# An FNet and MLP-mixer kernel: even-odd split of the feature transform, token-weight copies moved behind the fold of batch 1, fourth operand sum ahead of the third

## Chip, cores and metric

The kernel runs on one core of one Trainium2 chip. Times are device microseconds (us) of one execution. One run of the kernel before took 877 us at a clock of 0.66; it is left out.

## The reference

```python
# x (8, 3008, 256); w_tok1 (3008, 256); w_tok2 (256, 3008); w_ch1 (256, 1536); w_ch2 (1536, 256)
X = np.fft.fft(np.fft.fft(x, axis=1), axis=2).real        # token and feature transform
h = np.maximum(X.transpose(0, 2, 1) @ w_tok1, 0.0) @ w_tok2
u = X + h.transpose(0, 2, 1)
out = u + np.maximum(u @ w_ch1, 0.0) @ w_ch2
```

## The kernel before

TensorE does both transforms and all products in fp16. The work of a batch on the way to its output:

- **fold**: symmetric sums and differences of x, which halve the feature transform. VectorE does it for batches 0 and 1, GpSimd for the others, in steps placed between other work.
- **pz, z**: stage of the token transform. **pw, w**: the feature transform, 12 pairs of matmuls a batch. **py, pt, pu**: the rest of the token transform and the token MLP, up to `ut`.
- **mm1** (`pc`, ReLU into `c1`) and **mm2**, the channel MLP. A batch has six chunks of 512 tokens; a chunk has 12 "slots" (one per block of 128 hidden channels), here called slot 0 to 71 of a batch. mm2 uses seven block products instead of eight for most chunks; for that VectorE makes four operand sums `s` of 1536 fp16 elements a row per chunk.

The parts that the change and the argument touch (cuts marked):

```python
def fold(b, eng):                                   # 17 steps
    ...
    for t0, t1 in ((13, 17), (9, 13), (5, 9), (1, 5)):
        ...
        tt(fa[:], xp[:, t, 1:129], rv[:, :, 255:127:-1], AT.add, eng)
        yield
        tt(fb[:], rv[:, :, 1:129], xp[:, t, 255:127:-1], AT.add, eng)
        tt(eo[:, t, 0:1], xp[:, t, 0:1], rv[:, :, 0:1], AT.add, eng)
        yield
        tt(eo[:, t, 1:129], fa[:], fb[:], AT.add, eng)
        yield
        tt(eo[:, t, 129:256], fa[:, :, 0:127], fb[:, :, 0:127], AT.subtract, eng)
        yield
    ...
# feature transform, in front(b)
for g in range(NG):                                 # 12
    pw = ps_f("pw")
    nc.tensor.matmul(pw[:, 0:257], lhsT=zg[:, 1, g], rhs=td1[:], start=True, stop=False)
    nc.tensor.matmul(pw[:, 0:129], lhsT=zg[:, 0, g], rhs=td0[:], start=False, stop=True)
    copy(g % 2 == 0 and b == 0, w[:, g, :], pw[:, 0:257])
    yield
...
sum_at = {0: 1, 1: 2, 4: 3, 5: 4}                   # place in the chunk: which operand sum
places = {0: 0, 1: -1, 2: 1, 4: 2, 6: 3, 7: 4, 9: 5, 11: 6}   # which product
...
        if b == 0:
            if 12 <= slot < 24:
                take(fold1, 1 + slot % 2)           # fold of batch 1, on VectorE
            if slot == 21 and BB > 2:
                load_x(2)
            if slot in (22, 24, 26, 28):            # token weights into their later place, on GpSimd
                ...
                G.tensor_copy(out=w2r[:, th, 32 * hb:32 * hb + 32, 0:NQ], in_=...)
        ...
        if slot in fold_at:                         # fold of batch b + 2, on GpSimd
            ...
            G.tensor_copy(out=hold[:], in_=pbox[4][:, 0, 0, 0:1])   # waits for the fourth sum
            take(fold2, fold_at[slot])
```

`hold` is a copy of one column. Its only use is that GpSimd waits there until VectorE has the last sum of the chunk, so that the two don't meet.

## Time and profile before

| | before |
|---|---|
| median of the 3 runs | 604.52 us (603.12 to 604.69) |
| span of the profiled run | 601.9 us |
| first steady mm1 matmul, last matmul (starts) | 33.89 us, 597.80 us |
| TensorE from the one to the other | 563.91 us |

The last row is the one to think with: ahead of it lies a start-up that fills TensorE only in part, and behind it 4.1 us of last eviction (the copy of a result out of PSUM) and store. First, busy time by stretch (columns: window, its length, then busy us of PE, PEld, DVE, ACT, POOL, each with its instructions; granted clock, DMA share, GB/s):

```profile
64.00:110.00 46.00, 46.00 (x483) 32.66 (x482) 36.11 (x69) 28.11 (x56) 19.13 (x24) 1.00 0.32 73
...
180.00:250.00 70.00, 70.00 (x789) 50.88 (x787) 53.09 (x99) 47.00 (x93) 23.43 (x32) 1.00 0.56 91
```

TensorE has no idle time in either. Next, the timeline of GpSimd's token-weight copies and of the first operand sums that VectorE makes (start, us, engine, line, operation):

```profile
57.90 5.59 POOL L817 COPY w2r<-w2n 128x1504 f16<-128x1504 f16 x4
...
68.35 0.95 DVE L90 TENSOR_TENSOR s<-c 128x1536 f16<-128x1536 f16 x1
```

The copies end at 63.49 us, 4.9 us before the kernel's first sum. A sum takes 0.95 us. Last, the timeline around the third sum (`s<-c`) and the product that reads it (`pa<-t3w,s`), late in batch 0:

```profile
100.64 0.95 DVE L90 TENSOR_TENSOR s<-c 128x1536 f16<-128x1536 f16 x1
...
102.11 0.95 DVE L90 TENSOR_TENSOR s<-c,s 128x1536 f16<-128x1536 f16 x1
...
103.20 0.83 PE L650 MATMUL pa<-t3w,s 128*128 128x128 f16 x12
```

The third sum is there 1.6 us before its product.

### The profile page before, as it was taken

The numbers are of one execution on the slowest core, as the hardware profiler recorded it, in microseconds if no ns is written. First come the engines' busy times: TensorE is split into PE (matmuls) and PEld (weight loads), VectorE is DVE, ScalarE is ACT, GpSimd is POOL, SyncE is SP. The second block draws the span as 40 slices with busy tenths as digits, with TensorE's granted clock in tenths as the row PEclk, the third lists the DMA queues.
The fourth block names the chain that finished last, engine by engine and source line by source line (L and its number), as shares of the span: only waits on it lengthen the run. The fifth ranks groups of instructions, "written<-read, shape, count | busy, mean of one in ns | idle before, by whom it ended". The sixth has DMA issues, their size and how long they took to land.

```text
span 601.9 us, 15073 instructions
## 1 busy us (share of the span) xinstructions
PE 586.4 (97%) x6229; PEld 420.1 (70%) x6229; DVE 438.1 (73%) x884; ACT 387.2 (64%) x751; POOL 184.6 (31%) x260
## 2 busy tenths in 40 slices
PE   3999999999999999999999999999999999999997
PEld 2656676677667776667767777667766777666775
DVE  8778669566887578765888658856688757866663
ACT  8765665586657865577656866468665876546662
POOL 8443245603552143503336033450454000000000
PEclk9899999999999999999999999999999999999999
DMA  8994713671239812592336942376124533233433
GB/s 156 210 180 81 169 37 67 131 120 45 54 71 149 119 45 59 103 157 54 83 70 98 138 78 54 67 157 102 36 54 81 93 56 56 50 88 74 94 71 90
DMA packets 83381, 55.66 MB, mean 92 GB/s; under 512 B 53747, under 2 KB 80051, under 8 KB 82547
## 3 DMA queue, kind: packets, MB, share of 16 engines
q1 hardware_dynamic: 76816, 36.82, 32.6%
q0 software_dynamic: 6176, 17.63, 16.5%
q8 instruction: 48, 0.79, 0.5%
q10 hardware_dynamic: 320, 0.26, 0.2%
q14 instruction: 21, 0.16, 0.1%
HBM read 35.26 MB, written 24.64 MB: 100 GB/s over the span
## 4 chain that ended last, share of the span: by engine, by line
PE 95%; ACT 2%; DVE 2%; DMA 1%; issue 0%; DVEq 0%
PE pc L600 40%; PE pa L650 18%; PE pb L650 14%; PE pu L504 7%; PE po L705 5%; PE pt L533 3%; PE py L476 2%; PE pw L450 2%; PE pz L424 2%; DMA xm<-in_x_dram,ix 1%; PE pw L452 1%; ACT z L97 1%; ACT tts L97 0%; DVE yt L90 0%; DVE eo L90 0%; ACT w L97 0%
## 5 line engine op out<-in xcount | busy, mean ns | idle before, releaser
L97 ACT ACTIVATE c<-pc 128x512 f16<-128x512 f32 (+1 forms) x553 | 311.6, 590 | 154.7 <-PE pc L600 130.3
L600 PE MATMUL pc<-ut,wc 128*128 128x512 f16 (+1 forms) x1152 | 312.7, 374 | 0.3 <-DVE ut L90 0.3
L650 PEld LDWEIGHTS <-s 128*128 128x128 f16 x1968 | 123.4, 98 | 37.8 <-DVE s L90 1.5
L600 PEld LDWEIGHTS <-wc 128*128 128x128 f16 x1152 | 98.0, 98 | 57.0 <-issue 2.2
L650 PEld LDWEIGHTS <-c 128*128 128x128 f16 x1476 | 93.1, 97 | 27.8
L90 DVE TENSOR_TENSOR q<-pa,uT 128x256 f32<-128x256 f32 x123 | 53.1, 432 | 45.3 <-PE pa L650 44.5
L90 DVE TENSOR_TENSOR s<-c 128x1536 f16<-128x1536 f16 x82 | 78.8, 961 | 5.5 <-ACT c L97 5.5
L826 POOL COPY hold<-s 128x1 f16<-128x1 f16 x23 | 4.3, 188 | 251.3 <-DVE s L90 251.3
L90 DVE TENSOR_TENSOR osb<-pb,q 128x256 f32<-128x256 f32 x123 | 52.1, 424 | 33.4 <-PE pb L650 29.7
L90 DVE TENSOR_TENSOR ut<-pu,yt 128x512 f16<-128x512 f32 (+1 forms) x96 | 64.2, 674 | 2.3 <-PE pu L504 2.1
L90 POOL TENSOR_TENSOR eo<-fa,fb 96x512 f16<-96x512 f16 (+1 forms) x48 | 54.2, 1151 | 0.0
L504 PE MATMUL pu<-w2r,uu 128*128 128x512 f16 (+1 forms) x168 | 50.0, 379 | 0.0
L97 ACT ACTIVATE w<-pw 128x257 f16<-128x257 f32 x90 | 34.6, 385 | 10.6 <-PE pw L452 9.3
L90 DVE TENSOR_TENSOR s<-c,s 128x1536 f16<-128x1536 f16 x41 | 38.9, 949 | 0.0
L90 DVE TENSOR_TENSOR s<-s,c 128x1536 f16<-128x1536 f16 x41 | 38.8, 947 | 0.0
L705 PE MATMUL po<-wc,c 128*128 128x256 f16 x288 | 35.4, 273 | 0.0
L90 DVE TENSOR_TENSOR osb<-pa,uT 128x256 f32<-128x256 f32 x41 | 17.4, 425 | 23.7 <-PE pa L650 23.7
L650 PE MATMUL pb<-wc,c 128*128 128x128 f16 x492 | 34.4, 219 | 0.0
L650 PE MATMUL pa<-wc,c 128*128 128x128 f16 x492 | 34.4, 219 | 0.0
L650 PE MATMUL pa<-t2w,s 128*128 128x128 f16 x492 | 34.2, 219 | 0.0
L650 PE MATMUL pa<-t4w,c 128*128 128x128 f16 x492 | 34.2, 219 | 0.0
L650 PE MATMUL pb<-t1w,s 128*128 128x128 f16 x492 | 34.2, 219 | 0.0
(165 smaller groups left out, 672.5 us busy)
## 6 DMA issues: line engine op xcount, KB each, us to landing
out_dram<-osb SPq DMA_DIRECT2D x83, 256.0 KB
xp<-in_x_dram POOLq DMA_DIRECT2D x14, 408.0 KB, 10.2
out_dram<-osb SPq DMA_DIRECT2D x11, 192.0 KB
uT<-ut SPq DMA_TRANSPOSE x96
w2n<-in_moe_w_tok_dram POOLq DMA_DIRECT2D x2, 752.0 KB, 11.6
w1p<-in_moe_w_tok_dram POOLq DMA_DIRECT2D x2, 384.0 KB, 8.0
wc<-in_moe_w_ch_dram POOLq DMA_DIRECT2D x1, 768.0 KB
xp<-in_x_dram POOLq DMA_DIRECT2D x2, 272.0 KB, 6.6
```

Of the source, the lines that this page charges most:

```text
L90: eng.tensor_tensor(out=out_, in0=a, in1=b, op=op)
L97: nc.scalar.activation(out=out_, in_=in_, func=func, scale=scale, **kw)
L424: nc.tensor.matmul(pz[:, 96 * k:96 * k + 96], lhsT=eo[:, t0 + k, c], rhs=t1r, start=True, stop=True)
L450: nc.tensor.matmul(pw[:, 0:257], lhsT=zg[:, 1, g], rhs=td1[:], start=True, stop=False)
L452: nc.tensor.matmul(pw[:, 0:129], lhsT=zg[:, 0, g], rhs=td0[:], start=False, stop=True)
L476: nc.tensor.matmul(py[:, P * k:P * k + P], lhsT=w[:, 4 * c + k, o:o + P], rhs=tab[:, 4 * c + k, :], start=True, stop=True)
L504: nc.tensor.matmul(pu[:, 0:64 * nk], lhsT=uu[:, th, h, :], rhs=w2[:, th, :, 8 * c:8 * c + nk], start=(th == 0), stop=(th == 1))
L533: nc.tensor.matmul(pt[:, o:o + n], lhsT=hw[:, g, c], rhs=w[:, g, w0:w0 + n], start=(g == 0), stop=(g == NG - 1))
L600: nc.tensor.matmul(pc[:, 0:n], lhsT=wc1[:, h, ct * P:(ct + 1) * P], rhs=ut[:, c, h, 0:n], start=(h == 0), stop=(h == 1))
L650: nc.tensor.matmul(dst[:, P * a:P * a + P], lhsT=left[:, k, a, :], rhs=right[:, k, :], start=(first and k + a == 0), stop=(k == NH - 1), s ...
L705: nc.tensor.matmul(po[:, o:o + D], lhsT=c1[:, ct, ks * P:ks * P + P], rhs=wc2[:, ct, 0:D], start=(ct == 0), stop=(ct == NCT - 1))
L826: G.tensor_copy(out=hold[:], in_=pbox[4][:, 0, 0, 0:1])
```

## The change

Its intent: the feature transform is split once more into even and odd outputs, so a pair of matmuls has 2x65 + 2x64 = 258 columns instead of 257 + 129 = 386. The fold must deliver the even and odd parts and grows from 17 to 26 steps; so it is spread over more chunks. The fold of batch 1 gets 18 slots instead of 12, the front of each next batch starts somewhat later, and the token-weight copies and the load of batch 2's x move behind it. The fourth sum comes ahead of the third and `hold` waits for the third, so that GpSimd gets a longer stretch. The core of the diff:

```diff
-            nc.tensor.matmul(pw[:, 0:257], lhsT=zg[:, 1, g], rhs=td1[:],
-                             start=True, stop=False)
-            nc.tensor.matmul(pw[:, 0:129], lhsT=zg[:, 0, g], rhs=td0[:],
-                             start=False, stop=True)
+            nc.tensor.matmul(pw[:, 0:256].rearrange("p (h d) -> p h d", h=2)[:, :, 0:65],
+                             lhsT=zg[:, 0, g],
+                             rhs=td[:, 0:130].rearrange("p (h d) -> p h d", h=2),
+                             start=True, stop=True, skip_group_check=True)
+            nc.tensor.matmul(pw[:, 64:322].rearrange("p (h d) -> p h d", h=2)[:, :, 0:64],
+                             lhsT=zg[:, 1, g],
+                             rhs=td[:, 130:258].rearrange("p (h d) -> p h d", h=2),
+                             start=False, stop=True, skip_group_check=True)
 ... (in the fold, per group of four rows, behind fa and fb:)
+            for k in range(2):
+                parts(k, st[:, :, 0], st[:, :, 1], st[:, :, 0], st[:, :, 1], fa[:], fb[:], eng)
+                yield
+            if b:
+                tt(eo[:, t, 0:128], st[:, :, 0, 0:128], st[:, :, 1, 0:128], AT.add, eng)
+                yield
+                tt(eo[:, t, 128:256], st[:, :, 0, 1:129], st[:, :, 1, 1:129], AT.subtract, eng)
+                yield
 ... (batch 0 leaves these last two to TensorE, by accumulation; e128 goes, row 0 gets pad rows;
 ...  wc1 is loaded and the output sums are read in the new feature order)
-    NFOLD = 17
+    NFOLD = 26
-    sum_at = {0: 1, 1: 2, 4: 3, 5: 4}
+    sum_at = {0: 1, 1: 2, 3: 4, 4: 3}
-                    if 12 <= slot < 24:
+                    if 12 <= slot < 30:
                         take(fold1, 1 + slot % 2)
-                    if slot == 21 and BB > 2:
+                    if slot == 29 and BB > 2:
                         load_x(2)
-                    if slot in (22, 24, 26, 28):
-                        th, hb = (slot - 22) // 4, (slot - 22) // 2 % 2
+                    if 30 <= slot < 34:
+                        th, hb = (slot - 30) // 2, slot % 2
                         G.tensor_copy(out=w2r[...], in_=w2v[0][...])
-                if slot in fold_at:
 ...
+                if ct == 5 and (left or done >= 8):
 ...
+                        if joins:
+                            G.tensor_copy(out=hold[:], in_=pbox[3][:, 0, 0, 0:1])
+                        n = min(left, 6 if c == 5 or b < 2 else 5)
+                        take(fold2, n)
+                        left -= n
+                        if left == 0 and folding + 1 < BB:
+                            load_x(folding + 1)
```

## The prediction

> **What bounds the kernel now.** I began with the page: the busy line, the slices and the chain that ended last.
>
> ```profile
> PE 586.4 (97%) x6229; PEld 420.1 (70%) x6229; DVE 438.1 (73%) x884; ACT 387.2 (64%) x751; POOL 184.6 (31%) x260
> ...
> PE   3999999999999999999999999999999999999997
> ...
> PEclk9899999999999999999999999999999999999999
> ...
> PE 95%; ACT 2%; DVE 2%; DMA 1%; issue 0%; DVEq 0%
> ```
>
> TensorE works without a gap behind the first slice, at full clock, and carries 95% of the chain. Since busy matmul time alone proves little, I asked for busy time by stretch: between 60 and 540 us TensorE is busy in every microsecond, and its 15.6 us of idle time lie in the first 30 us (10.7), between 30 and 60 us (about 1.0) and after 570 us (3.9). In the middle a microsecond of matmul columns taken away is a microsecond of time, unless another engine then fails to keep up. The others' load differs by stage:
>
> ```profile
> 40.00:50.00 10.00, 10.00 (x75) 6.51 (x73) 7.89 (x20) 6.53 (x14) 3.10 (x3) 1.00 0.65 89
> 50.00:60.00 10.00, 9.53 (x83) 6.21 (x82) 8.26 (x21) 5.83 (x11) 5.10 (x6) 1.00 0.55 85
> ...
> 95.00:110.00 15.00, 15.00 (x143) 9.93 (x141) 13.90 (x26) 7.29 (x14) 7.60 (x10) 1.00 0.30 63
> 110.00:180.00 70.00, 70.00 (x758) 50.41 (x756) 50.44 (x97) 45.10 (x89) 25.27 (x37) 1.00 0.45 91
> ```
>
> (Columns: window, its length, then busy us of PE, PEld, DVE, ACT, POOL.) VectorE is at 80% where it folds batch 1, at 93% late in batch 0, yet TensorE stays full there; from batch 1 on VectorE is at 72%.
>
> What the feature transform costs TensorE I read from the order of instructions, because a matmul's own 270 ns holds pipeline latency that overlaps its neighbours:
>
> ```profile
> 126.13 0.59 PE L600 MATMUL pc<-ut,wc 128*128 128x512 f16 x2
> 126.56 0.27 PE L450 MATMUL pw<-td,z 128*128 128x257 f16 x1
> 126.67 0.22 PE L452 MATMUL pw<-td,z 128*128 128x129 f16 x1
> 126.73 0.59 PE L600 MATMUL pc<-ut,wc 128*128 128x512 f16 x2
> ```
>
> Start to start, 257 columns take 0.11 us and 129 take 0.06: a pair occupies 0.17 us.
>
> **What the Trainium skill says.** "TensorE: Matmul & The Clock Gate", section "Back-to-back issue gap", gives N/2.4 + 2.5 ns for a warm isolated matmul and some 81 ns for N=128 in a stream with a weight load each. The trace agrees with the first: 24 matmuls of 129 and 127 columns, each with its weight load, stand in the chain as 1.36 us, 56.7 ns each (128/2.4 + 2.5 = 55.8). The 81 ns are not seen here, so halving a matmul to 128 columns really halves its cost. "SBUF — State Buffer", section "Who interferes with whom", says that a VectorE instruction with two SBUF inputs contends with a GpSimd instruction that reads SBUF, and that whichever is second fully blocks. The trace agrees once: VectorE's fa of batch 1 started at 41.73 and took 1.65 us instead of 0.42, while GpSimd's t4w ran from 41.56 to 43.10. This is why the kernel has the one-column copy `hold`: it lets GpSimd fold only after VectorE's four operand sums of a chunk. "PSUM — Partial Sum Buffer", section "The four PSUM rules", says that the starting matmul clears the written bits of the whole zero region and later ones overwrite where the bit is clear. The new second matmul relies on that, for it touches columns that the first has not written. That bears on correctness; no run here shows it yet.
>
> **The change part by part.**
>
> 1. The pair of the transform goes from 257+129 = 386 columns to 2x65 and 2x64 = 258 columns, without another instruction. 128 columns at 2.4 per ns are 53 ns; 12 groups times 8 batches are 96 pairs: 96 x 53 ns = 5.1 us. 84 pairs lie in the full middle; the 12 of batch 0 lie between 18.7 and 24.9 us, where TensorE is nearly full too.
>
> 2. The correction matmul with e128 goes (one per batch), and row 0 now takes two 24-column matmuls per half instead of one: batches 1 to 7 get one small matmul more each. Row 17.25 to 17.28 shows 0.03 us for one: 7 x 0.03 = +0.2 us.
>
> 3. Batch 0 does not do the final sums in its fold; TensorE does them by accumulation. 30 more matmuls of 96 columns at 0.044 us (five span 0.38, of which 0.206 is the last one's own time) are 1.3 us, and 7 small ones 0.2. They stand at 12.9 to 17.7 us, where TensorE waits for VectorE's fold and ScalarE's z copies. I take a third as visible, 0.5 us; more ScalarE set-up (four short table instructions in place of two of 0.48 and 0.38) makes it +0.6 us.
>
> 4. The fold on GpSimd (batches 2 to 7) grows from 17 to 26 steps. Before, one costs (27.7+27.6+27.5+27.5+5.2+3.3+2.6+2.6+1.1)/6 = 20.9 us. The durations fit 0.19 us + 1.88 ns per element (128 elements 0.43, 512 elements 1.15), so 256 elements should take 0.67. A group of four rows becomes 1.15+1.15+0.22 + 4 x 0.67 + 2 x 1.15 = 7.5 us; four groups 30 us and row 0 some 2.8: about 33 us. Six folds: +72 us, POOL to about 257 us. None is on the path by itself. The question is collision. Before, the sums run 201.62 to 208.01 and the next chunk's begin at 214.11, leaving some 6.1 us to a fold of 4.7 us. With the fourth sum before the third the last ends about one slot (1 us) sooner, leaving about 7.1 us for five steps of about 6.2 us, or six of 7.5. So five fit and six overrun by about half a microsecond, which lands on the next chunk's first sum. That sum's product is needed only three slots later. I count +0.3 us.
>
> 5. The fold of batch 1 stays on VectorE. Per group it had 4 x 0.415 + 0.16 = 1.8 us and gets 2 x 0.415 + 0.16 + 4 x 0.28 + 2 x 0.415 = 2.9 (0.28 between 128 elements in 0.216 and 512 in 0.415): 8.0 us become 13.4, with row 0. That is +5.4 us on an engine with about 4 us to spare in 40 to 60 us. The change gives it 18 slots rather than 12, about 5 us more room, so it is just full. +0.5 us for evictions that come late to TensorE.
>
> 6. x of batch 2 is now asked for at slot 29, one chunk ahead of its fold, where it had some 20 us. Its rows took 8.4 us from issue to landing, others' 7.6 to 15.3. A late one only shifts GpSimd's fold into the next sums: +0.2 us, for it happens in batches 0 to 2 alone.
>
> 7. The token-weight copies move with the fold; 5.6 us on an idle GpSimd either way: 0. The output sums in permuted feature order have the same element counts and float32 PSUM inputs: 0. Each plain output eviction gets a third tiny instruction (0.1 to 0.2 us), which shows once, at the end: +0.1.
>
> Sum: -5.1 + 0.2 + 0.6 + 0.3 + 0.5 + 0.2 + 0.1 = -3.2 us, 604.5 - 3.2 = 601.3 us.
>
> **The rivals.** (a) GpSimd's longer fold blocks VectorE. For it: the 1.65 us fa, and 7.5 us of steps in a 7 us room. Against: the blocked instruction loses at most one GpSimd instruction, 1.15 us, and where VectorE was 93% busy TensorE still never waited. If it held in each of about 27 chunks with a fold and TensorE lost half a microsecond, +13 us: about 615. (b) Everything else hides as intended, batch 0's extra matmuls included: -5.1 + 0.2, 599.6 us. (c) The strided PSUM output of the halves costs TensorE more than a contiguous one, say as much as it saves: then 606. Against it: the stream's matmuls into quarters of a bank already run at 56 ns, though none here writes two separate blocks. (d) VectorE saturates in the fold of batch 1: 5.4 us of work with no room, up to +4 us more: 605.
>
> **Range and chances.** The saving is arithmetic on a full engine; the give-backs are estimates of 2 us that may be 0.5 or 5. Hence 598.6 to 604.2 us. Faster by over 2% needs 592.4, more than twice what was taken from TensorE: 0.02. Slower by over 2% needs 616.6, that is rival (a) in full: 0.03. Within 2%: 0.95.
>
> **What would show it.** Step 1: start to start, the new pair takes 0.11 us, and its matmuls stand at the 130- and 128-column forms. Step 3: the first steady mm1 matmul (33.89 us before) comes between 33.3 and 34.5. Step 4: a POOL row near 257 us; the mean of the 1536-element sums stays under 1.05 us (0.961, 0.949 and 0.947 before); a DVE instruction that runs over 2 us during a fold would speak for (a), and so would idle time of PE between 110 and 540 us above 1 us. Step 5: DVE over 95% busy between 42 and 64 us and PE idle there of about 1 us. Step 6: GpSimd's fa of batch 2 waiting for x. My prediction is wrong if PE idles in the middle for more than 2 us, or if a pair costs 0.14 us or more.

## The result, and the profile after

| | before | changed |
|---|---|---|
| median, first comparison (4 runs each) | 603.86 us (603.12 to 604.69) | 602.88 us (602.36 to 603.38) |
| ratio, 95% interval | | 0.9983 (0.9964 to 1.0003) |
| span of the profiled run | 601.9 us | 600.3 us |
| first steady mm1 matmul, last matmul | 33.89, 597.80 us | 33.92, 596.17 us |
| TensorE from the one to the other | 563.91 us | 562.25 us |

A ratio here is the mean time of one kernel's fast runs over that of the other's in the same rounds, so not quite the ratio of the medians. The time fell by about 1 us (0.17%) where 3.2 us were forecast: it lies in the range and in the class "within 2%", but two thirds of the expected gain are missing. By the interval of the ratio the gain may be anything from 0 to 2.2 us; in the two profiled runs, on which the account below rests, it is 1.7 us behind the start-up, and half is missing. The page of the changed kernel, its busy line and its row of the operand sums that read `c` alone (count | busy us, mean ns | idle before):

```profile
PE 583.2 (97%) x6273; PEld 417.3 (70%) x6273; DVE 452.8 (75%) x924; ACT 387.3 (65%) x753; POOL 259.3 (43%) x396
...
L90 DVE TENSOR_TENSOR s<-c 128x1536 f16<-128x1536 f16 x82 | 82.0, 1000 | 4.7 <-ACT c L97 4.7
```

GpSimd's 259.3 us are what was predicted (257); these sums' mean went from 961 to 1000 ns. The two stretches shown of before, after:

```profile
64.00:110.00 46.00, 45.28 (x475) 31.38 (x474) 38.87 (x69) 27.31 (x55) 26.67 (x35) 1.00 0.42 87
...
180.00:250.00 70.00, 69.56 (x789) 50.13 (x787) 54.67 (x100) 46.90 (x92) 36.78 (x58) 1.00 0.57 92
```

TensorE is idle 0.72 and 0.44 us where it was idle for nothing, although no other engine is over 85% busy. From the start times of the matmuls one sees more than from busy time. I took each matmul's distance to the next start and subtracted columns/2.4 + 2.5 ns (the form that the prediction held against the trace); what is left is waiting. Between the first mm1 matmul and the last it is 4.8 us before and 7.6 us after, so +2.7 us of waits and small losses stand against 4.4 us of columns taken away: -1.7 us. By stretch:

| stretch, us | before | changed |
|---|---|---|
| 34 to 64 | 1.51 | 1.53 |
| 64 to 110 | 0.52 | 1.95 |
| 110 to 180 | 0.53 | 0.71 |
| 180 to 250 | 0.30 | 1.13 |

Behind 250 us the two differ by some 0.25 us, all small. The single waits of 0.1 us or more behind 64 us that are new (two of 0.11 us, at 118.2 and 542.2, aside) lie at 71.6 and 72.8 us (0.58 + 0.18 us), at 89.9 and 104.1 us (0.30 + 0.32), at 144.2 (0.10), 183.3 (0.56) and 230.0 us (0.20): 2.24 us. Three kinds of them can be seen in timelines of the changed kernel. The first:

```profile
64.62 5.58 POOL L898 COPY w2r<-w2n 128x1504 f16<-128x1504 f16 x4
...
67.93 3.08 DVE L90 TENSOR_TENSOR s<-c 128x1536 f16<-128x1536 f16 x1
...
70.93 0.61 DVE L90 TENSOR_TENSOR ut<-pu,yt 128x448 f16<-128x448 f32 x1
...
71.59 0.64 PE L566 MATMUL pu<-w2n,uu 128*128 128x448 f16 x2 [0.42 <-DVE ut L90]
...
72.80 0.84 PE L712 MATMUL pa<-t2w,s 128*128 128x128 f16 x12
```

The copies that ended at 63.49 us before now run until 70.20, into the first operand sum, which takes 3.08 us instead of 0.95. It ends at 71.01, 0.8 us after the last of them. Behind it on VectorE `ut` is late, for which TensorE waits at 71.59, and so is the second sum, for which it waits at 72.80. The second kind:

```profile
101.26 0.94 DVE L90 TENSOR_TENSOR s<-c,s 128x1536 f16<-128x1536 f16 x1
...
103.06 0.94 DVE L90 TENSOR_TENSOR s<-c 128x1536 f16<-128x1536 f16 x1
...
104.06 0.84 PE L712 MATMUL pa<-t3w,s 128*128 128x128 f16 x12 [0.15 <-DVE s L90]
```

No sum is slow here. The fourth stands in front of the third, two evictions stand between them, and the product starts as soon as the third is there, 0.3 us late. The third kind:

```profile
179.58 2.87 POOL L90 TENSOR_TENSOR eo<-sab 96x512 f16<-96x512 f16 x2
...
181.78 1.48 DVE L90 TENSOR_TENSOR s<-s,c 128x1536 f16<-128x1536 f16 x1
...
183.32 0.84 PE L712 MATMUL pa<-t2w,s 128*128 128x128 f16 x12 [0.40 <-DVE s L90]
```

A group of six fold steps reaches into the next chunk's sums: the second takes 1.48 us and its product waits. The pair itself, in the timeline of the changed kernel, against 0.11 and 0.06 us before:

```profile
142.98 0.22 PE L508 MATMUL pw<-td,z 128*128 128x130 f16 x1
143.04 0.22 PE L512 MATMUL pw<-td,z 128*128 128x128 f16 x1
143.10 0.59 PE L662 MATMUL pc<-ut,wc 128*128 128x512 f16 x2
```

Averaged over the 84 pairs behind 34 us: 109.9 + 56.6 ns became 56.6 + 60.8 ns, 49.1 ns less.

### The profile page after: what moved, and what is told of

Read it like the earlier page. It is cut to its first block, busy times and chain, and to the rows that moved or that the text cites. A ratio compares the mean times of both kernels' runs of the same rounds, so it can differ in the third digit from the quotient of the medians.

```text
span 600.3 us, 15332 instructions
## 1 busy us (share of the span) xinstructions
PE 583.2 (97%) x6273; PEld 417.3 (70%) x6273; DVE 452.8 (75%) x924; ACT 387.3 (65%) x753; POOL 259.3 (43%) x396
## 4 chain that ended last, share of the span: by engine, by line
PE 81%; DVE 1%; issue 0%; ACT 0%; DVEq 0%
PE pc L662 35%; PE pa L712 17%; PE pb L712 13%; PE pu L566 5%; PE po L775 4%; PE pt L595 3%; PE pz L471 1%; PE py L538 1%; DVE s L90 1%; PE pw L508 1%; PE pw L512 1%; DVE osb L90 0%; DVE q L90 0%; DVE ut L90 0%; ACT c L97 0%
## 5 line engine op out<-in xcount | busy, mean ns | idle before, releaser
L90 DVE TENSOR_TENSOR s<-c 128x1536 f16<-128x1536 f16 x82 | 82.0, 1000 | 4.7 <-ACT c L97 4.7
L90 POOL TENSOR_TENSOR eo<-sab 96x512 f16<-96x512 f16 x48 | 53.9, 1139 | 1.6
L90 POOL TENSOR_TENSOR sab<-fa,fb 96x256 f16<-96x256 f16 (+1 forms) x72 | 46.7, 673 | 0.0
L90 DVE TENSOR_TENSOR s<-s,c 128x1536 f16<-128x1536 f16 x41 | 41.1, 1003 | 0.0
L712 PE MATMUL pa<-t3w,s 128*128 128x128 f16 x492 | 34.2, 219 | 0.3 <-DVE s L90 0.2
```

Source lines behind the costliest of these rows:

```text
L90: eng.tensor_tensor(out=out_, in0=a, in1=b, op=op)
L712: nc.tensor.matmul(dst[:, P * a:P * a + P], lhsT=left[:, k, a, :], rhs=right[:, k, :], start=(first and k + a == 0), stop=(k == NH - 1), s ...
```

## The experiments

**Theory.** The pair saves nearly what was forecast; 1.9 of its 4.1 us behind the start-up are given back in operand sums on VectorE that come late, by three causes: the token-weight copies meet the first sum (0.76 us), the new sum order puts the third sum behind the fourth (0.61 us), and six fold steps overrun (0.56 us). **Rivals.** The new pair is slower than its columns, for instance by its output in separate blocks; or the longer fold costs VectorE a little everywhere, and the single waits are incidental.

Start-up and the landing of batch 1's x move by some tenths from run to run, so beside the times I give the **later stretch**: from the start of the last small `pz` matmuls of batch 1 (61.77 us in the changed kernel) to the start of the last matmul. In the changed kernel it is 534.40 us, in a repeat of it 534.71 (there the wait near 144 us is 0.41 instead of 0.10 us). Each value is of one trace, so a difference counts where the waits that it should remove are seen to go. "Mm1 to end" is the stretch of the tables above.

**The pair alone.** The kernel before with the two new matmuls, on wrong tables and an unchanged fold, so its result is wrong (relative error 0.94) and nothing else differs.

```diff
-  pw[:, 0:257] = zg[:, 1, g] x td1;  pw[:, 0:129] += zg[:, 0, g] x td0
+  the two matmuls of the changed kernel, with rhs td1[:, 0:130] and td1[:, 129:257]
```

> The kernel before with nothing changed but the shape of the transform's two matmuls (65+65 and 64+64 columns into separate blocks; the result is wrong on purpose). This is the saving alone, with fold, sums and copies as before. Theory (the saving came in nearly full and was given back by new waits): a pair falls from 166 ns to about 117 ns start to start, so 84 pairs in the full stretch save 4.1 us and the 12 of batch 0 up to 0.6 us: about 599.5 us, ratio 0.992 to 0.994. Rival (the saving never came, because narrow matmuls cost more than their columns or because another engine limits the middle): ratio 0.997 to 1.000, like the changed kernel's 0.9983.

Measured: 600.01 us, ratio 0.9927 (0.9914 to 0.9940), 4.4 us under the median before it (604.39). 56.6 + 61.6 ns a pair. Mm1 to end took 561.37 us, with an extra wait of 1.25 us at 51.3 us in the profiled run. That wait goes with a late x of batch 1 (fold from 42.60 us, 41.73 before). From the last `pz` matmuls of batch 1 to the end it took 535.68 us, against 539.64 before: 3.96 us less. The saving comes; the pair is not what eats it.

**Why the second matmul of the pair takes 5 ns more than its columns.** Three single looks, each the pair alone with one thing altered, all wrong on purpose: the output in one unbroken stretch of columns; the second table read from an even 256-byte boundary; the two matmuls swapped.

```diff
-  outputs pw[:, 0:65] + pw[:, 128:193] and pw[:, 64:128] + pw[:, 193:257]
+  pair_flat:    outputs pw[:, 0:130] and pw[:, 130:258]
-  second rhs td1[:, 129:257]
+  pair_aligned: second rhs td1[:, 128:256]
-  130 columns first, 128 second
+  pair_swap:    128 columns first, 130 second
```

> The kernel before with the transform's two matmuls in 130 and 128 columns, as in the run of the pair alone, but each written to one unbroken stretch of PSUM, the two side by side (result wrong on purpose). In the changed kernel and in the pair alone the first takes 56.6 ns start to start, what its columns give, and the second 61, 5 ns more than its 128 columns. If the broken and overlapping output is what costs, the second takes 56 here; if it is the narrow width or the place in the stream, it stays at 61.

> As the run with the pair alone (wrong on purpose), but the second matmul reads its 128 table columns from an even 256-byte boundary instead of from column 129. If the 5 ns extra of the second matmul come from where its moving operand starts: it takes 55.8 ns to the next start instead of 60.8 to 61.6. If they come from the position (a 128-column matmul ahead of the mm1 matmul of 512 columns), nothing changes: 60.8 or more.

> As the run with the pair alone (wrong on purpose), but with the 128-column matmul first and the 130-column one second. If the extra 5 ns belong to the 128-column matmul and its operand: 60.8 first and 56.6 second. If they belong to standing second, ahead of the 512-column mm1 matmul: 55.8 first and 61 to 62 second.

Measured: 599.49, 599.28 and 599.93 us, one run each. To the next start, first and second matmul: flat 56.4 and 60.8 ns, aligned 56.6 and 60.8, swapped 56.6 and 61.2. The timeline of the swapped one, with start times to 0.01 us:

```profile
124.38 0.22 PE L450 MATMUL pw<-td,z 128*128 128x128 f16 x1
124.44 0.22 PE L454 MATMUL pw<-td,z 128*128 128x130 f16 x1
```

Whichever stands second takes 4.5 to 5.8 ns more than columns/2.4 + 2.5; layout and boundary change that by 0.8 ns at most (61.6 against 60.8). In the kernel before the second matmul, 129 columns behind 257, took 56.6 ns and paid nothing. The extra is worth 84 x 5 ns = 0.4 us. Why it comes is open, and the place alone, behind a short matmul and ahead of mm1, is not the cause: in the changed kernel's trace the last of four `py` matmuls ahead of mm1 takes 56.0 ns, and the last of the 12 of a product 55.8 to 55.9, so 12 short ones in a row pay nothing either.

**The copies apart.** The changed kernel, with two copies where they were and two behind the sums of the fourth chunk, in place of three fold steps.

```diff
-                    if 30 <= slot < 34:
-                        ...
+                    if slot in (30, 31):
+                        copy_w2(0, slot - 30)
 ... (at the fold)
+                        if b == 0 and c == 3:
+                            copy_w2(1, 0); copy_w2(1, 1)
-                        n = min(left, 6 if c == 5 or b < 2 else 5)
+                        n = min(left, 3 if b == 0 and c == 3 else 6 if c == 5 or b < 2 else 5)
```

> The changed kernel with two of the four token-weight copies left at slots 30 and 31 and the other two moved behind the operand sums of the fourth chunk, where they take the room of three fold steps. Theory (the copies on GpSimd held up the first operand sum, 3.08 us instead of 0.95 at 67.9 us, and TensorE waited 0.76 us for it at 71.6 and 72.8 us): that sum takes about 0.95 us, both waits go, and the span falls by 0.6 to 0.8 us against the changed kernel, to a ratio near 0.997. Rival (TensorE waited there for the denser front of batch 1, not for the sum): the sum is short again, but TensorE still loses about as much between 68 and 75 us and the time stays at 602.9.

Measured: 602.75 us, 0.9979 (0.9966 to 0.9992): no gain over the changed kernel; later stretch 534.51. The waits at 72 us and the one at 104 us are gone, and others are there at 157.2 (0.18), 174.2 (0.63) and 347.2 us (0.53). GpSimd's timeline in this run shows where the first comes from:

```profile
128.91 1.11 POOL L106 DMA_DIRECT2D xp<-in_x_dram  x2
...
134.42 0.18 POOL L910 COPY hold<-s 128x1 f16<-128x1 f16 x1 [0.47 <-DVE s L90]
139.15 1.14 POOL L90 TENSOR_TENSOR fa<-xp,xm 96x508 f16<-96x508 f16 x1 [4.55 <-DMA xm<-in_x_dram,ix]
```

Three steps less in one chunk end batch 2's fold later, so batch 3's x is asked for at 128.9 instead of 126.2 us; its fold waits 4.55 us for x behind `hold` and then runs into the next sums, of which the second takes 1.03 us and the fourth 1.48. The other two don't follow from this timeline: at 174.2 us TensorE waits for the third sum behind the fourth, with no fold step running, and the fold's wait for x ahead of 347.2 us (1.37 us) was there in the changed kernel too (1.50 us, in its repeat none) and cost nothing. So the mend for one collision moved the load that starts behind it and made one other; how the rest came is open. The theory of the collision itself is neither refuted nor shown by this run's time.

**The copies on another engine.** Two copies stay on GpSimd at slots 30 and 31; the other half goes to ScalarE in four pieces. The fold and the loads keep their places.

```diff
-                    if 30 <= slot < 34:
-                        ...
+                    if slot in (30, 31):
+                        hb = slot - 30
+                        G.tensor_copy(out=w2r[:, 0, 32 * hb:32 * hb + 32, 0:NQ], in_=...)
+                    if slot in (28, 30, 32, 34):
+                        q = (slot - 28) // 2
+                        act(w2r[:, 1, 16 * q:16 * q + 16, 0:NQ], w2v[0][:, 1, 16 * q:16 * q + 16, :])
```

> The changed kernel with two of the four token-weight copies at slots 30 and 31 on GpSimd, as in the change, and the other two cut into four pieces on ScalarE (slots 28 to 34), so that GpSimd's fold and its loads of x keep their times. The run with the split copies took the two waits at 71.6 and 72.8 us away but held back x of batch 3 by 3 us, and new waits of 0.18, 0.63 and 0.53 us came. Theory (the copies cost 0.76 us by the held sum, and the rest of that run's loss came from x landing late): the first sum takes about 0.95 us, the waits near 72 us go, those at 157, 174 and 347 us do not come, and the stretch from the first steady matmul to the last is 561.4 to 561.7 us (562.25 in the changed kernel). Rival (any shift of GpSimd's schedule by these copies brings waits elsewhere): 562.0 us or more.

Measured: 601.66 us, 0.9963 (0.9949 to 0.9976). Mm1 to end took 561.43 us, in the range expected; the later stretch is 533.58, that is 0.82 us less than in the changed kernel. The timeline:

```profile
64.91 2.82 POOL L898 COPY w2r<-w2n 128x1504 f16<-128x1504 f16 x2
...
68.22 0.95 DVE L90 TENSOR_TENSOR s<-c 128x1536 f16<-128x1536 f16 x1
```

GpSimd is done at 67.73, the first sum takes 0.95 us again, and no matmul waits at 72 us. So the collision costs the 0.8 us that it was said to.

**The third sum first again.** Places 3 and 4 keep their sums, in the old order; `hold` waits for the fourth.

```diff
-    sum_at = {0: 1, 1: 2, 3: 4, 4: 3}
+    sum_at = {0: 1, 1: 2, 3: 3, 4: 4}
-                            G.tensor_copy(out=hold[:], in_=pbox[3][:, 0, 0, 0:1])
+                            G.tensor_copy(out=hold[:], in_=pbox[4][:, 0, 0, 0:1])
```

> The changed kernel with the third operand sum at place 3 and the fourth at place 4, so both are still done as early as in the change, but in the old order. Theory (putting the fourth sum ahead made the product that needs the third wait while VectorE is full, late in batch 0): the two waits ahead of that product at 89.9 and 104.1 us, 0.30 and 0.32 us, go, and the span falls by 0.5 to 0.6 us. Rival (VectorE was simply late there, whatever the order): the waits stay, or come back at another product, and the time stays at 602.9.

Measured: 602.44 us, 0.9974 (0.9961 to 0.9988). The waits at 89.9 and 104.1 us are gone and the later stretch is 533.80, 0.60 us less. Mm1 to end shows only 0.13 us (562.12), because in this run x of batch 1 landed later, its fold on VectorE began at 42.27 instead of 41.56 us, and the wait near 53 us was 0.67 instead of 0.21 us. The place shown above, with the third sum, the fourth, and the product:

```profile
100.90 0.94 DVE L90 TENSOR_TENSOR s<-c 128x1536 f16<-128x1536 f16 x1
...
102.70 0.94 DVE L90 TENSOR_TENSOR s<-c,s 128x1536 f16<-128x1536 f16 x1
...
104.09 0.83 PE L712 MATMUL pa<-t3w,s 128*128 128x128 f16 x12
```

GpSimd lost nothing by it. From the end of a chunk's last sum to the next chunk's first there are 7.0 us on average in both kernels, 6.2 before the change and 6.3 in the next run: the room comes from the earlier places, not from the order.

**The sums where they were before.** Old order and old places, all else as changed.

```diff
-    sum_at = {0: 1, 1: 2, 3: 4, 4: 3}
+    sum_at = {0: 1, 1: 2, 4: 3, 5: 4}
     (hold waits for pbox[4])
```

> The changed kernel with the four operand sums back at the old places (first, second, third, fourth at 0, 1, 4, 5) and the copy that releases the fold behind the fourth again: this undoes the third part of the change alone. Theory (the new order made the product with the third sum wait in batch 0, but lets the fold start a slot sooner): the waits at 89.9 and 104.1 us, 0.61 us in sum, go, and the fold runs about 1 us later into the next chunk's sums, so waits at the product with the second sum grow from 0.56 us to 1 us or more in batches 1 and 2; in sum no gain or a loss of up to 2 us, that is 602.3 to 604.5. Rival (the earlier start of the fold is worth nothing): the span falls by 0.5 to 0.6 us as with the third sum first.

Measured: 604.34 us, 1.0005 (0.9992 to 1.0019), all of the gain lost; later stretch 536.15, 1.75 us more. The two waits for the third sum are gone; three new ones appear, at 149.8, 205.5 and 331.7 us (0.23, 0.43 and 0.84 us), and the one near 230 us grows from 0.20 to 0.99 us. That one in the timeline:

```profile
226.31 1.30 POOL L90 TENSOR_TENSOR sab<-fa,fb 96x256 f16<-96x256 f16 x2
226.92 1.50 DVE L90 TENSOR_TENSOR s<-c 128x1536 f16<-128x1536 f16 x1
...
230.87 0.84 PE L712 MATMUL pa<-t2w,s 128*128 128x128 f16 x12 [0.83 <-DVE s L90]
```

Here, and at 205.5 us, the fold starts later in its chunk and meets the next sums (1.50 instead of 0.95 us). The waits at 149.8 and 331.7 us are of another kind: they stand ahead of the fifth product, which reads no sum, and wait for the eviction `q` of VectorE.

```profile
331.18 0.42 DVE L90 TENSOR_TENSOR q<-pa,uT 128x256 f32<-128x256 f32 x1 [1.49 <-PE pc L662]
...
331.65 0.83 PE L712 MATMUL pa<-t4w,c 128*128 128x128 f16 x12 [0.68 <-DVE q L90]
```

At 331 us GpSimd does not even fold, and why `q` came only behind an mm1 matmul is open. The early places are worth 1.75 us against the order of the change and 2.35 us against the run with the third sum first, which differs from this one in the places alone; about 1 us of it is a fold that does not fit, 1.07 us are these two waits. The time lay in the range of my forecast (602.3 to 604.5), but its reason holds for half of the loss.

**Five fold steps instead of six in the last chunk of batch 1**, the chunk ahead of the wait at 183.3 us.

```diff
-                        n = min(left, 6 if c == 5 or b < 2 else 5)
+                        n = min(left, 5 if b == 1 and c == 5 else 6 if c == 5 or b < 2 else 5)
```

> The changed kernel with five fold steps instead of six in the last chunk of batch 1; the one left over moves into the first chunk of batch 2, which has three then. Theory (GpSimd's sixth step ran into the next chunk's second operand sum, 1.48 us instead of 0.95, and TensorE waited 0.56 us at 183.3 us): the sum takes about 0.95 us, the wait goes and the span falls by 0.4 to 0.6 us. Rival (the wait belongs to the turn from batch 1 to 2, where VectorE's queue is long anyhow): a wait of over 0.3 us stays within 2 us of that place.

Measured: 603.12 us, 0.9991 (0.9974 to 1.0008): nothing gained; later stretch 534.32. The wait at 183.3 us is gone, so six steps did cause it. But one step more in a later chunk puts the load of batch 4's x off from 188.0 to 189.3 us (0.6 us of that because all of this run lies later), and then:

```profile
198.38 1.14 POOL L90 TENSOR_TENSOR fa<-xp,xm 96x508 f16<-96x508 f16 x1 [1.12 <-DMA xm<-in_x_dram,ix]
...
204.39 1.48 DVE L90 TENSOR_TENSOR s<-s,c 128x1536 f16<-128x1536 f16 x1
...
205.93 0.84 PE L712 MATMUL pa<-t2w,s 128*128 128x128 f16 x12 [0.24 <-DVE s L90]
```

The fold waits for x, and the same kind of wait returns one chunk on (0.41 us by start times).

**Two and three mends together, and the changed kernel in the same rounds.** The second mended kernel has, beside the third sum first and half the copies on ScalarE, its own number of steps for each chunk. Both give the right result.

```diff
 two_mended:   the edits of "the third sum first again" and "the copies on another engine"
 three_mended: these, and
-                        n = min(left, 6 if c == 5 or b < 2 else 5)
+                        n = min(left, (6 if b == 0 or c < 5 else 5) if b < 2
+                                else (6, 4, 5, 5, 6, 6)[c])
```

> A version meant to beat both kernels: the changed kernel with the third sum ahead of the fourth (both at the early places), half of the token-weight copies in pieces on ScalarE, five fold steps at the end of batch 1, and from batch 2 on 4, 5, 5, 6 and 6 steps in chunks 1 to 5 in place of 5, 5, 5, 5 and 6, so that a first chunk that has to wait for x does not run on into the sums. Theory (the three waits are separate losses of 0.76, 0.61 and about 0.5 us): the stretch from the first steady matmul to the last is 560.3 to 560.9 us, and the time about 601.0, ratio 0.994 to 0.996. Rival (a wait taken away comes back at the next place where GpSimd or VectorE is late): 561.5 us or more, ratio 0.997.

> The changed kernel with two mends alone: half the token-weight copies on ScalarE and the sums in the order 1, 2, 3, 4; the fold's steps per chunk as in the changed kernel. If these two carry the gain and the table of steps is worth little, as the run with five steps at the turn suggests: 601.1 to 601.7 us, ratio about 0.995 to 0.996, a wait of about 0.5 us near 183 us, none at 72, 90 and 104. If the steps matter as much as the collision they remove (0.56 us): 601.7 or more.

> The changed kernel itself, unaltered, in the same rounds as the mended one, because the step from it to the mended kernels was so far only compared across two sets of rounds. If the gain of about 1 us is real and not a matter of the day: 602.5 to 603.3 us, ratio to before 0.998. If the other calls' kernels were merely luckier with their runs: about 601.7.

Measured: three mends 601.12 us, 0.9949 (0.9936 to 0.9963); two mends 601.22 us, 0.9956 (0.9943 to 0.9969); the changed kernel again 602.84 us, 0.9991 (0.9975 to 1.0007), in the same rounds as the two mends. So the mends are worth 1.6 us in one set of rounds, and not a matter of luck with the runs. Stretches of the one with three:

```profile
64.00:110.00 46.00, 46.00 (x488) 32.71 (x487) 36.78 (x72) 29.17 (x59) 26.17 (x35) 1.00 0.43 90
...
180.00:250.00 70.00, 69.91 (x795) 50.47 (x792) 54.44 (x100) 47.07 (x93) 35.62 (x58) 1.00 0.52 92
```

TensorE is full again from 64 to 110 us, and idle for 0.09 instead of 0.44 us from 180 to 250. The later stretch gives a sum that closes:

| kernel | later stretch, us | against the changed one |
|---|---|---|
| changed (repeat) | 534.40 (534.71) | |
| third sum first | 533.80 | -0.60 |
| copies on ScalarE | 533.58 | -0.82 |
| both | 533.00 | -1.40 |
| both and the steps | 532.50 | -1.90 |

Two mends give the sum of their single values (0.60 + 0.82 = 1.42), which speaks for separate causes and against a general loss. The third is worth 0.5 us in the trace; in time its ratio is lower by 0.0007, well within the intervals. The mends win back 1.9 of the roughly 2.4 us that the change gives back behind the start-up (4.1 us of the pair less 1.66). Not mended is a start-up loss: in the profiled runs with two and three mends batch 1's x landed late (fold from 42.50 and 42.95 us) and TensorE waited 1.47 and 0.94 us near 53.6 us, so that mm1 to end with three mends was 561.08 us where 560.3 to 560.9 were expected. That wait was 0.2 us in the changed kernel and in all other kernels with its order of sums or its old places, and 0.67 with the third sum first alone. All three with the third sum first at the early places have it, then; but the pair alone, with a late x too, waited 1.25 us, and the first sum runs only at 68 us. So I put it down to the landing and not to the mends; that is not shown, and what moves the landing was not tested.

## Why the prediction was wrong where it was

Term by term, predicted against what the traces show:

| step of the prediction | forecast | measured |
|---|---|---|
| 1 the shorter pair | -5.1 | -4.1 behind 34 us; at -49.1 ns for each of 96 pairs -4.7 |
| 2 the pad rows | +0.2 | +0.2 |
| 3 batch 0's sums on TensorE | +0.6 | some +0.5 (first steady mm1 at 34.12 us on average over the nine traces with the new fold, 33.6 over the four with the new pair alone; single traces differ by up to 0.9) |
| 4 fold of batches 2 to 7 on GpSimd | +0.3 | about +0.9 (0.56 at 183, 0.10 at 144, 0.20 at 230) |
| 5 fold of batch 1 on VectorE | +0.5 | 0 in this profile, more where x came late |
| 6 later load of x | +0.2 | 0 |
| 7 copies, output sums, evictions | +0.1 | copies +0.8; nothing seen of the rest |
| the new sum order (counted only as room for the fold) | in 4 | +0.6 |

Behind 34 us: -4.1 + 0.2 + 0.9 + 0.8 + 0.6 = -1.6, against the measured -1.66 us. Ahead of it step 3 and the 12 early pairs (12 x 49 ns = 0.6 us) about cancel. Of the 3.2 us forecast, 1.5 are missing in these traces: 0.8 for the copies, 0.6 for the order of sums, 0.6 for step 4 and 0.4 for step 1, less 0.8 that steps 5 to 7 had counted and that did not come.

**The step that failed is the seventh**: "5.6 us on an idle GpSimd either way: 0". I looked at how busy GpSimd was and not at what VectorE would do at those slots. The copies moved from slots 22 to 28, ahead of the first chunk with operand sums, to 30 to 33, from where they run into slot 36, where those sums begin. I had the rule in hand, wrote it into step 4 for the fold, and did not apply it to the copies. With it fell the argument against rival (a), that "the blocked instruction loses at most one GpSimd instruction": the sum lost 2.1 us across two copies of 1.43 us. That the copies were the cause is shown by the run with half of them on ScalarE.

**Step 4 had the mechanism right and two sizes off.** Steps, durations and GpSimd's total came as worked out (a 256-element part 0.673 us, forecast 0.67), and six steps overran, as said, but by 1.9 and not half a microsecond: ahead of 180.6 us the room was 6.2 us and not 7.1. "That sum's product is needed only three slots later" was wrong: it was the second sum that was slowed, whose product stood waiting. And the swap of sums was only counted as an earlier end, which it does not bring: the room is 7.0 us in either order. That the third comes later for its own product, at two places where VectorE is over 90% busy, cost 0.6 us; the run with the old order at the new places shows it. The early places were right to take (with the old ones 1.75 us are lost), the swap was not.

**Step 1** was right within a tenth: a step of 53 ns was 49 ns, because the matmul that stands second takes 60.8 ns and not 55.8. That the second matmul may write columns which the first has not, as the prediction read in the Trainium skill ("PSUM — Partial Sum Buffer", section "The four PSUM rules"), now has a run that agrees: the changed kernel's result is correct. Rival (c), a slow strided output, is refuted by the unbroken one at the same 60.8.

**Step 5**: VectorE was as full as forecast, yet TensorE didn't wait for it more than before. Its window, in the changed kernel:

```profile
50.00:60.00 10.00, 9.96 (x84) 6.55 (x82) 10.00 (x30) 4.88 (x9) 0.00 (x0) 1.00 0.34 79
```

VectorE full for 10 us was no wait for TensorE here. But there is little slack: with x 0.7 us later, as in the run with the third sum first, TensorE waited 0.5 us more.

The test that I set, idle time of TensorE of over 2 us in the middle, did not fire (some 1.2 us from 64 to 540 us), and the gain was gone anyway: a 128-column matmul counts as busy for 0.22 us where the next starts after 0.06, so busy time hides part of each wait. Distances between starts would have been the better test.

## What to carry to other kernels

When work moves in a schedule, ask for each moved instruction which instructions of the engine that shares its memory run at the new place; "that engine is idle" is no answer. On an engine that is full for 500 us, a saving of 5 us is as big as a dozen waits of 0.4 us, so find them by the distance between starts and not by busy time, and mend them by moving work to a third engine where it triggers nothing: two mends that moved GpSimd's own steps put off the load behind them, and a wait came back elsewhere. Order sums by which product reads which first; here the other order brought no earlier end and cost 0.6 us.

## What the Trainium skill lacked or had wrong

- "SBUF — State Buffer", section "Who interferes with whom", says that whichever of VectorE and GpSimd comes second is blocked. It does not say who gets the memory between two GpSimd instructions in a row. Here a waiting sum was passed over: it started at 67.93 us, one copy ended at 68.81 and the next, begun at 68.76, ran to 70.20; the sum took 3.08 instead of 0.95 us. Elsewhere the turn did pass: near 180.6 us a fold step took 1.85 instead of 1.06 us while a sum of 0.94 us ran.
- "TensorE: Matmul & The Clock Gate", section "Back-to-back issue gap": the 81 ns for N=128 and the 131 ns for N=512 in a stream were not seen (some 56 ns in the products, 216 in mm1). But the second of the two short matmuls of a pair took 60.8 to 61.6 ns ahead of a 512-column one, whatever its layout or operand; no page explains that.
- "Perfetto Trace Analysis", section "Identifying the Most-Contended Engine", warns that matmul busy time does not show how near a kernel is to the roofline. It does not say that a wait of TensorE is partly hidden too: from 64 to 110 us TensorE's idle time by busy records grew by 0.72 us, by the distances of starts by 1.43 us.
